# Four pairs of q and k loads, one transposing load and a record load moved in the queues of an attention and mixture-of-experts kernel

## The chip, the cores and the metric

The kernel runs on one core of a Trainium2 chip. The metric is the time of one execution in device microseconds (us). A core has five engines with instruction queues of their own: TensorE (PE in the rows, its weight loads PEld), VectorE (DVE), ScalarE (ACT), GpSimd (POOL) and SyncE (SP). Transfers are started by GpSimd or SyncE and carried out by the 16 DMA engines that the two share.

## The reference

A block-causal attention over 8 batches, 8 heads, 576 rows and head size 64, and on its output a router that sends each of 4608 tokens to two of eight experts:

```python
scores = scale * np.matmul(q, k.transpose(0, 1, 3, 2))      # masked by 64-row blocks
attn = softmax(scores); x = (attn @ v) as [4608, 512]
noisy_logits = x @ w_gate + log1p(exp(x @ w_noise)) * noise
top2, top2_w = two largest of 8, softmax over the two
for e in range(8):
    for k in range(2):
        mask = top2[:, k] == e
        out[mask] += top2_w[mask, k, None] * (relu(x[mask] @ w1[e]) @ w2[e])
```

## The kernel before

**Stages.** The attention goes over four pairs of batches (`g` from 0 to 3). For each pair q and k arrive in five chunks (`load_qk`, chunks 4, 0, 1, 2, 3, each 256 KB but chunk 4), are transposed by TensorE (L439, L444) and copied by VectorE (L460). The scores of a pair are 26 steps (L525, L532, L541), with an exponential on ScalarE after each (L551, L553), then come two sets of nine products with v (L600, L614), which VectorE divides and writes into a row buffer `xr` (L621, L622). The pairs alternate between two such buffers. TensorE then transposes the rows and makes the logits, VectorE ranks the tokens, and `scatter` (L790) sends each row of 512 values and an 8-value record to its expert's region of the DRAM array `xd`, 18 scatters for each pair. Named by the plan, they are `D0.0` to `D0.17` for pair 0, `D1.0` to `D1.17` for pair 1, and so on. Pair 2's division of tile `idx` writes where `D0.2*idx` and `D0.2*idx+1` read, and so waits for these two scatters alone.

Pairs 0 and 1 fill `xd[0]`, pairs 2 and 3 fill `xd[1]`. Each half is then eight buckets, one for each expert with 640 rows, 16 buckets in all (`b` from 0 to 15). For a bucket `load_x` (L934) reads its rows with one transposing DMA into one of three buffers (`xg0`, `xg1`, and `xT`, which lies where the logits' tiles were); buckets 0 and 1 come in tiles instead (L942). TensorE multiplies by w1 (L1017) and w2 (L1033), ScalarE applies the relu (L1023) and copies the result out (L1040, L1042) into one of ten tiles, and SyncE stores each, 128 KB, to `yd` (L1049). GpSimd gathers rows (L1056) and writes the results of the second half (L1075). Weights come by GpSimd's queue (L910, L912).

The records of the second half are read back from `xd[1]` in one transfer of 16-byte pieces (`load_rec`, L974) by SyncE. VectorE works out from them, from L984 on, the weights and addresses that the second half needs.

**Order.** A planner (`Plan`) simulates the engines from written costs and due times and gives one order for everything. Each engine takes its instructions in that order. A transfer may also wait for another that it does not read: each of the two queues marks its transfers on eight semaphores in turn, so one waits until the eighth before it in its queue has landed. `due` of an `LX` step is its place in time for the planner; `LX6.0` is bucket 6, the seventh of the first half.

Of the kernel before, what the change touches and what calls it, by code (L numbers as in the profile page):

```python
# [11 lines left out]
I32 = mybir.dt.int32  # L12
# [200 lines left out]
def kernel(  # L213
# [12 lines left out]
    nc = tc.nc  # L226

    B, H, S, D = q.shape
    N, Dm = out.shape
    E = moe_w_gate.shape[1]  # L230
    F = moe_w1.shape[2]
    assert Dm == H * D and N == B * S
    P = 128
    DB = Dm // P
    FB = F // P
    NG = B // 2
# [4 lines left out]
    CAP = 640  # L241
# [4 lines left out]
    OVB = E * CAP  # L246
    XR = OVB + 2 * TH * P
    DR = Dm + 8
# [12 lines left out]
    xd = [nc.dram_tensor(f"xd{i}", (XR, DR), BF16, kind="Internal").ap() for i in range(NH)]  # L261
# [58 lines left out]
    rc = low.tile([P, E, CT, 4], I32, name="rc")  # L320
# [22 lines left out]
    pl = Plan()  # L343
# [68 lines left out]
    for g in range(NG):  # L412
        for ch in (4, 0, 1, 2, 3):
            for nm in "qk":
                pl.add(f"L{nm}{g}.{ch}", {"POOL": 0.58 if ch == 4 else 0.74}, lambda e, g=g, nm=nm, ch=ch: load_qk(g, nm, ch),
                       due=due_u(g, first_u[ch]) - (18.,18.,18.,22.)[g] + (0.1 if nm == "k" else 0) - (3 if ch == 4 else 0),
                       take=[("r" + nm, ("raw", g, nm, ch))], dma=0.7 if ch == 4 else 1.41, packet=88)
        for i in range(6):
            pl.add(f"V{g}.{i}", {"POOL": 1.18 if i < 4 else 0.7}, lambda e, g=g, i=i: load_v(g, i),
                   due=due_u(g, 6) - (8. if g else 16.) + i * 0.2, rel=0.0 if g < 1 else due_u(g, 0) - 8.,  # L420
                   take=[("vt", ("vt", g))] if i == 0 else [], deps=[f"V{g}.0"] if i else [],
# [55 lines left out]
    for g in range(NG):  # L477
        for nm in "qk":
            for ch in ("4B", 0, 1, 2, 3, "4A"):
# [4 lines left out]
                else:  # L484
                    need, u, lh = [f"L{nm}{g}.{ch}"], first_u[ch], last_h[ch]
                due = due_u(g, u) - 4 + (0.1 if nm == "k" else 0)
# [4 lines left out]
                       take=[("bk", ("tp", g, nm, ch), 1 if g else 0)], free=fr, lat=0.25)  # L491
# [4 lines left out]
                if ch == 0:  # L496
                    pl.add(f"CW{nm}{g}", {"DVE": 0.12}, lambda e, g=g, nm=nm: wrap(g, nm, e),
                           deps=[f"T{nm}{g}.0"] + ([s_name(g - 1, 7)] if g else []), due=due + 0.6, lat=0.15)
                pl.add(f"C{nm}{g}.{ch}", on,
                       lambda e, g=g, nm=nm, ch=ch: turned(g, nm, ch, e), deps=[f"T{nm}{g}.{ch}"] + prev,  # L500
                       due=due + 0.5, free=[("tp", g, nm, ch)], lat=0.15)
# [67 lines left out]
    for g in range(NG):  # L569
        for u in range(UG):  # L570
            st, w = divmod(u, UN)
            hs = [st * SET + w // 3] if w < UN - 1 else range(st * SET, st * SET + SET)
            need = {f"C{nm}{g}.{c}" for h in hs for c in chunks_of(h) for nm in "qk"}
            if 0 in hs:
                need |= {f"CW{nm}{g}" for nm in "qk"}
            small = w == UN - 1
            take = [("sc", ("sc", g, u))]
            pl.add(f"Q{g}.{u}", {"PE": 0.15 if small else (0.26, 0.3, 0.33)[w % 3]},
                   lambda e, g=g, u=u: score(g, u), mode="64*64" if small else "64*128",
                   deps=sorted(need) + ["masks"], due=due_u(g, u), take=take, lat=0.25)  # L580
            pl.add(f"S{g}.{u}", {"ACT": 0.48 if small else 1.0}, lambda e, g=g, u=u: exps(g, u),
                   deps=[f"Q{g}.{u}"], due=due_u(g, u), free=[("sc", g, u)],
                   take=[("esc", ("esc", g, st))] if w == 0 else [], lat=0.2)
# [42 lines left out]
    for g in range(NG):  # L626
        for st in range(2):
            need = [f"S{g}.{st * UN + w}" for w in range(UN)] + [f"V{g}.{i}" for i in range(6)] + ["vones"]
            for idx in range(TG):
                n = 0.75 if idx == 8 else 0.02 + (idx % 4 + 1) * 0.118  # L630
                due = due_u(g, (st + 1) * UN) + 1 + idx * 1.3 - LEAD[g]
                pl.add(f"A{g}.{st}.{idx}", {"PE": n}, lambda e, g=g, st=st, idx=idx: av(g, st, idx),
                       deps=need, due=due, take=[("bk", ("av", g, st, idx))], mode="128*64" if idx == 8 else "128*128",
                       free=[("esc", g, st), ("vt", g)], lat=0.25)
                pl.add(f"N{g}.{st}.{idx}", {"DVE": 0.62}, lambda e, g=g, st=st, idx=idx: av_out(g, st, idx),
                       deps=[f"A{g}.{st}.{idx}"] + ([f"N{g}.0.0"] if (st, idx) != (0, 0) else []), due=due + 0.3,
                       free=[("av", g, st, idx), ("rden", g, st, idx)],
                       take=[("rden", ("rden", g, st, idx))]
# [169 lines left out]
    for half in range(NH):  # L808
        pl.add(f"Z{half}", {"SP": 0.7}, lambda e, half=half: clear_x(half),
               due=due_u(half, 14), rel=due_u(half, 14), deps=["vones"], dma=2.5, packet=165, anchor=True)  # L810

    for g in range(NG):
        half, r0 = g // 2, due_u(g, UG) + 6 - LEAD[g]
        for j in range(5):
# [4 lines left out]
                   take=[("bk", ("xt", g, j))], lat=0.25)  # L819
            pl.add(f"XC{g}.{j}", {"DVE": 0.1 + 0.26 * n, "ACT": 0.12 + 0.44 * n},  # L820
                   lambda e, g=g, j=j: x_turned(g, j, e), deps=[f"X{g}.{j}"], due=d + 0.5,
                   take=[("xT", ("xT", g, j))], free=[("xt", g, j)], lat=0.2)
            pl.add(f"G{g}.{j}", {"PE": 0.11 * n}, lambda e, g=g, j=j: logits(g, j), mode="128*128",
                   deps=[f"XC{g}.{j}", "wgn"] + ([f"G{g}.0"] if j else []) + ([f"R{g - 1}.rows"] if g else []),
                   due=d + 1, take=[("bk", ("lg", g))] if j == 0 else [], free=[("xT", g, j)], lat=0.25)
# [9 lines left out]
               deps=[f"R{g}.cnt", "consts"] + ([f"R{g - 1}.room"] if g else []), due=r1 + 4, free=[("lg", g)])  # L835
        pl.add(f"R{g}.room", {"DVE": 0.4}, lambda e, g=g: room(g), deps=[f"R{g}.rows"], due=r1 + 14)
        pl.add(f"R{g}.keep", {"DVE": 0.6 if g < NG // 2 else 0.2}, lambda e, g=g: keep(g), deps=[f"R{g}.w1", f"R{g}.rows"], due=r1 + 14, free=[("xr", g)])
        for j in range(2 * TG):
            pl.add(f"D{g}.{j}", {"POOL": 1.28}, lambda e, g=g, j=j: scatter(g, j),
                   deps=[f"R{g}.rows", f"R{g}.w1", f"R{g}.tok", f"Z{half}"],  # L840
                   due=(r1 + 7 - 10. if g < NG // 2 else 180. if g == NG - 1 else 150.) + j * 0.9,
# [80 lines left out]
    for e in range(E):  # L922
        b0 = e
        for which in (1, 2):
            for part in range(2):
                deps = freed(e, which)
                pl.add(f"W{which}.{e}.{part}", {"POOL": 0.8}, lambda x, e=e, w=which, p=part: load_w(e, w, p),
                       deps=deps, due=(w_rel[e] if e in w_rel else bucket_due(b0) - 20.) + 4 * which + 2 * part,
# [33 lines left out]
    def rows_of(gs):  # L962
        return [f"D{g}.{j}" for g in gs for j in range(2 * TG)]

    def rows_landed(ins, half, gs):
        own = [i for g in gs for i in scat[g]]
        apart(ins, f"scat{half}", own)
        for i in own:
            tc.add_manual_dep(ins.ins, i.name, SYNC_DEP, reason="rows landed")
        member(ins, f"rows{half}")  # L970
        return ins

    def load_rec():
        ins = nc.sync.dma_start(out=rc.rearrange("p e c w -> p (e c) w"),  # L974
                                in_=xd[1].bitcast(I32)[0:OVB, Dm // 2:DR // 2].rearrange("(c p) w -> p c w", p=P))
        return rows_landed(ins, 1, [2, 3])

    def read_rec():
        f = [rc[:, :, :, i].bitcast(I32 if i == 3 else F32) for i in range(4)]
# [130 lines left out]
    for b, i in ORDER:  # L1110
        half, e = SEQ[b]
        c0, n = PIECES_OF[b][i]
        d0, nb = DUE[(b, i)], step_of(b, i)
        if b < EARLY:
            for c in range(c0 // P, (c0 + n) // P):
                pl.add(f"LX{b}.{c}", {"SP": 0.4}, lambda x, b=b, c=c: load_tile(b, c),
                       deps=rows_of(groups(b, c // 2)), due=d0 - 8 + c * 0.2, take=[("y", ("xl", b, c))], dma=0.4, packet=47)
                pl.add(f"XT{b}.{c}", {"PE": 0.23}, lambda x, b=b, c=c: turn_tile(b, c), mode="128*128", deps=[f"LX{b}.{c}"],
                       due=d0 - 3, take=[("bk", ("xp", b, c), 1)], free=[("xl", b, c)], lat=0.25)
                pl.add(f"XX{b}.{c}", {"DVE": 0.36, "ACT": 0.6}, lambda x, b=b, c=c: tile_turned(b, c, x),  # L1120
                       deps=[f"XT{b}.{c}"], due=d0 - 2, free=[("xp", b, c)], lat=0.2,
                       take=[("xg", ("xg", b))] if c == 0 else [])
                if c:
                    pl.ops[f"XX{b}.{c}"].deps.append(f"XX{b}.0")
        elif i == 0:
            pl.add(f"LX{b}.0", {"SP": 0.3}, lambda x, b=b: load_x(b),
                   deps=rows_of([2 * half, 2 * half + 1]), due=d0 - 12., take=[("xg", ("xg", b))],
                   dma=2.5, packet=22, hold=True, seq="xg")
        for st in range(FB // nb):
            d1 = d0 + st * nb * 0.55 * n / NW  # L1130
            deps = [f"XX{b}.{c}" for c in range(c0 // P, (c0 + n) // P)] if b < EARLY else [f"LX{b}.0"]
            deps = deps + [f"W1.{e}.{p}" for p in range(2)]
            pl.add(f"F1.{b}.{i}.{st}", {"PE": nb * max(0.545 * n / NW, 0.23)},
                   lambda x, b=b, i=i, st=st: layer1(b, i, st), deps=deps, due=d1, mode="128*128",
                   take=[("bk", ("hp", b, i, st), 1)] + ([("h", ("h", b))] if (i, st) == (0, 0) else []),
                   free=[("xg", b)], lat=0.25, seq="layer1")
            pl.add(f"RE.{b}.{i}.{st}", {"ACT": 0.16 + nb * n * 0.001}, lambda x, b=b, i=i, st=st: relu(b, i, st),
                   deps=[f"F1.{b}.{i}.{st}"], due=d1, free=[("hp", b, i, st)], lat=0.2)
        for c in range(CT):
# [6 lines left out]
            for kk in range(2):  # L1146
                deps = []
                for k in need:
# [4 lines left out]
                       due=d2 + kk * 0.87, take=[("bk", ("yp", b, c), 1)] if not kk else [],  # L1153
                       free=[("h", b)], lat=0.25)
            if half == 0 or e < E - 1:
                pl.add(f"Y.{b}.{c}", {"ACT": 0.73}, lambda x, b=b, c=c: keep_row(b, c),
                       deps=[f"F2.{b}.{c}.1"] + (["RR"] if half else []), due=d2 + 1, take=[("y", ("y", b, c))],
                       free=[("yp", b, c)])
                pl.add(f"YS.{b}.{c}", {"SP": 0.6}, lambda x, b=b, c=c: store_row(b, c), deps=[f"Y.{b}.{c}"],
                       due=d2 + 1.5, free=[("y", b, c)], dma=0.4, packet=48)  # L1160
            if half and e:
                deps = ["RR"] + [f"YS.{E + e2}.{c2}" for e2 in range(e) for c2 in range(CT)]
# [160 lines left out]
    pl.eng_free.update({"POOL": 1.5, "DVE": 1.6, "ACT": 2.0, "PE": 1.6, "SP": 1.0})  # L1323
    pl.run()

    reg = {n: nc.gpsimd.to_reg(n - 1) for n in [XR, N] + [e * CAP for e in range(1, E + 1)]}

    sched = tc.manual_schedule(engines={mybir.EngineType.PE, mybir.EngineType.Activation, mybir.EngineType.DVE,
# [122 lines left out]
```

## Time and profile before

| | us |
|---|---|
| median of 3 runs | 459.71 |
| lowest, highest | 459.61, 460.60 |
| the profiled execution, its own time | 462.31 |
| its span, first to last instruction | 460.5 |
| TensorE busy in the span | 400.1 |
| GpSimd busy | 260.1 |
| ScalarE busy | 256.0 |
| VectorE busy | 162.8 |

The profiled execution is one run, 2.60 us above the median; 1.81 us of its time lie outside its span. All times in rows are counted from the span's start. A row's bracket is how long its engine stood idle before it, and what ended that.

### The profile page before, as it was taken

The numbers are of one execution on the slowest core, as the hardware profiler recorded it, in microseconds if no ns is written. First come the engines' busy times: TensorE is split into PE (matmuls) and PEld (weight loads), VectorE is DVE, ScalarE is ACT, GpSimd is POOL, SyncE is SP. The second block draws the span as 40 slices with busy tenths as digits, with TensorE's granted clock in tenths as the row PEclk, the third lists the DMA queues.
The fourth block names the chain that finished last, engine by engine and source line by source line (L and its number), as shares of the span: only waits on it lengthen the run. The fifth ranks groups of instructions, "written<-read, shape, count | busy, mean of one in ns | idle before, by whom it ended". The sixth has DMA issues, their size and how long they took to land. (4 is left out here: it accounts for less than half of the span.)

```text
span 460.5 us, 10885 instructions
## 1 busy us (share of the span) xinstructions
PE 400.1 (87%) x4384; PEld 255.7 (56%) x4384; DVE 162.8 (35%) x451; ACT 256.0 (56%) x447; POOL 260.1 (56%) x293
## 2 busy tenths in 40 slices
PE   3899779869697999999899499999998998999950
PEld 3667666657456776555555165565554554655620
DVE  3768698877617510000000020023322423332320
ACT  2898687957791544745554154555554554655410
POOL 8756447877785775672120002433757777777760
PEclk9999999998999999999999799999999999999995
DMA  8999993999999799999999995758688477555430
GB/s 126 189 218 199 193 187 107 130 204 182 233 163 248 172 217 210 276 236 153 193 220 168 215 154 133 133 128 207 115 172 180 139 182 184 181 176 172 146 129 1
DMA packets 128073, 80.26 MB, mean 174 GB/s; under 512 B 85696, under 2 KB 115981, under 8 KB 128016
## 3 DMA queue, kind: packets, MB, share of 16 engines
q0 software_dynamic: 69856, 52.37, 67.3%
q1 hardware_dynamic: 58160, 27.14, 28.3%
q8 instruction: 36, 0.59, 0.5%
q14 instruction: 21, 0.17, 0.1%
HBM read 72.74 MB, written 35.17 MB: 234 GB/s over the span
## 5 line engine op out<-in xcount | busy, mean ns | idle before, releaser
L551 ACT ACTIVATE esc<-sc 128x1024 bf16<-128x1024 f32 x96 | 92.9, 1028 | 20.5 <-PE sc L532 20.0
L1033 PEld LDWEIGHTS <-h 128*128 128x128 bf16 x640 | 62.2, 98 | 72.7 <-issue 7.6
L790 POOL DMA_INDIRECT xd<-xr,slots x72 | 72.0, 1001 | 37.6 <-issue 17.3
L1023 ACT ACTIVATE h<-sc 128x320 bf16<-128x320 f32 (+1 forms) x120 | 49.6, 444 | 47.2 <-PE sc L1017 30.4
L1056 POOL DMA_INDIRECT xr<-yd,slots x36 | 36.8, 1021 | 66.5 <-DMA yd<-zero 44.8
L1023 ACT ACTIVATE h<-bk 128x320 bf16<-128x320 f32 (+1 forms) x124 | 55.7, 456 | 17.2 <-PE bk L1017 12.6
L1017 PEld LDWEIGHTS <-w 128*128 128x128 bf16 x448 | 40.8, 98 | 15.6 <-issue 1.3
L1017 PEld LDWEIGHTS <-esc 128*128 128x128 bf16 x384 | 37.5, 98 | 20.4 <-issue 3.1
L1056 POOL DMA_INDIRECT xr<-yd,grow x35 | 36.4, 1040 | 17.1 <-issue 9.8
L525 PE MATMUL sc<-qT,kT 64*128 64x512 bf16 (+4 forms) x320 | 37.9, 303 | 4.6 <-ACT esc L551 4.1
L984 DVE TENSOR_TENSOR rtmp<-rc,rowid 128x40 f32<-128x40 f32 x1 | 0.2, 226 | 99.1 <-DMA rc<-xd 99.1
L1033 PE MATMUL sc<-esc,h 128*128 128x512 bf16 x136 | 32.0, 379 | 2.2 <-DVE xr L1069 2.0
L1033 PE MATMUL bk<-w,h 128*128 128x512 bf16 x128 | 31.6, 379 | 0.8 <-DVE xr L1069 0.8
L600 PEld LDWEIGHTS <-esc 128*128 128x128 bf16 x640 | 23.9, 99 | 12.9 <-issue 11.0
L600 PE MATMUL bk<-vt,esc 128*128 128x65 bf16 x540 | 24.4, 197 | 4.3 <-DVE xr L622 1.4
L1033 PE MATMUL sc<-w,h 128*128 128x512 bf16 x112 | 27.6, 379 | 0.2 <-ACT h L1023 0.2
L1075 POOL DMA_INDIRECT out_dram<-xr,trow x21 | 21.4, 1019 | 10.0 <-issue 4.6
L460 DVE COPY kT<-bk 128x1024 bf16<-128x1024 bf16 (+1 forms) x24 | 24.9, 1041 | 5.8 <-PE bk L439 5.1
L1017 PE MATMUL sc<-xg,esc 128*128 128x320 bf16 x168 | 26.6, 299 | 0.4 <-ACT h L1023 0.3
L622 DVE TENSOR_TENSOR xr<-bk,rden 128x256 bf16<-128x256 f32 x61 | 25.9, 424 | 2.1
L1033 PE MATMUL bk<-esc,h 128*128 128x512 bf16 x104 | 24.9, 379 | 1.5 <-DMA esc<-in_moe_w_dram 1.5
L1017 PE MATMUL bk<-xg,esc 128*128 128x320 bf16 x152 | 24.4, 299 | 0.0
(212 smaller groups left out, 640.0 us busy)
## 6 DMA issues: line engine op xcount, KB each, us to landing
w<-in_moe_w_dram POOLq DMA_DIRECT2D x12, 512.0 KB
esc<-in_moe_w_dram POOLq DMA_DIRECT2D x12, 512.0 KB
yd<-xr SPq DMA_DIRECT2D x35, 128.0 KB
rq<-in_q_dram POOLq DMA_DIRECT2D x16, 256.0 KB
rk<-in_k_dram POOLq DMA_DIRECT2D x16, 256.0 KB
vt<-in_v_dram POOLq DMA_DIRECT2D x16, 256.0 KB
yd<-y SPq DMA_DIRECT2D x31, 128.0 KB
out_dram<-o SPq DMA_DIRECT2D x24, 128.0 KB
```

The source lines that it names most:

```text
L460: nc.vector.tensor_copy(o, i)
L525: nc.tensor.matmul(out=sc[:, hf, off:off + z - a], lhsT=kT[sl, c0 + jt * P:c0 + jt * P + P], rhs=qT[sl, c0 + a:c0 + z], start=True, stop=n ...
L551: return nc.scalar.activation(out=esc_t[i][:, hh, :, piece * 512:(piece + 1) * 512], in_=sc, func=AF.Exp, scale=scale)
L600: nc.tensor.matmul(out=a[:, hh, :], lhsT=esc[:, hh, hf, c:c + P], rhs=vb[:, jt, hf, h, 0:D + 1], start=(jt == 0), stop=(jt == ib))
L622: nc.vector.tensor_tensor(out=xr[:, idx, st * SET * D:(st + 1) * SET * D].rearrange("p (h d) -> p h d", h=SET), in0=a[:, :, 0:D], in1=rden ...
L790: ins = nc.gpsimd.indirect_dma_start(out=xd[half].bitcast(I32), out_offset=bass.IndirectOffsetOnAxis(ap=slots[:, g * TG + idx, i:i + 1], a ...
L984: vec.tensor_tensor(out=first, in0=f[0], in1=rowid, op=ALU.is_equal)
L1017: nc.tensor.matmul(out=hp[:, j * n:(j + 1) * n], lhsT=w1sb[:, db, fb * P:(fb + 1) * P], rhs=xg[:, db, c0:c0 + n], start=(db == 0), stop=(d ...
L1023: return nc.scalar.activation(out=h_t[pl.slot(("h", b))][:, s * nb:(s + 1) * nb, c0:c0 + n], in_=bank(("hp", b, i, s))[:, 0:nb * n].rearra ...
L1033: nc.tensor.matmul(out=yp, lhsT=h[:, fb, c * P:(c + 1) * P], rhs=w2sb[:, fb, :], start=(fb == 0), stop=(fb == FB - 1))
L1056: ins = nc.gpsimd.indirect_dma_start(out=g_t[pl.slot(key)], out_offset=None, in_=yd[half][0:len(es) * CAP, :], in_offset=bass.IndirectOffs ...
L1075: ins = nc.gpsimd.indirect_dma_start(out=out, out_offset=bass.IndirectOffsetOnAxis(ap=trow[:, e, c:c + 1], axis=0), in_=out_tile(("o", b, ...
```

## The change

Three edits. After the planner has made its order, the q and k loads of chunks 0, 1, 2 and 3 of the last pair are taken out and put ahead of the scatters `D0.13`, `D0.14`, `D0.16` and `D1.1`. Bucket 6's `LX` step has its due time 44 us ahead of the bucket's instead of 12. The record load becomes two transfers: three experts' records by GpSimd's queue, five by SyncE's.

```diff
     def load_rec():
-        ins = nc.sync.dma_start(out=rc.rearrange("p e c w -> p (e c) w"),
-                                in_=xd[1].bitcast(I32)[0:OVB, Dm // 2:DR // 2].rearrange("(c p) w -> p c w", p=P))
-        return rows_landed(ins, 1, [2, 3])
+
+        q = 3
+        for eng, e0, e1 in ((nc.gpsimd, 0, q), (nc.sync, q, E)):
+            ins = eng.dma_start(out=rc[:, e0:e1].rearrange("p e c w -> p (e c) w"),
+                                in_=xd[1].bitcast(I32)[e0 * CAP:e1 * CAP, Dm // 2:DR // 2].rearrange("(c p) w -> p c w", p=P))
+            rows_landed(ins, 1, [2, 3])
+        return ins
...
-                   deps=rows_of([2 * half, 2 * half + 1]), due=d0 - 12., take=[("xg", ("xg", b))],
+                   deps=rows_of([2 * half, 2 * half + 1]), due=d0 - (44. if b == 6 else 12.), take=[("xg", ("xg", b))],
...
     pl.run()
+
+    for ch, step in ((0, "D0.13"), (1, "D0.14"), (2, "D0.16"), (3, "D1.1")):
+        loads = [pl.ops[f"L{nm}{NG - 1}.{ch}"] for nm in "qk"]
+        pl.order = [o for o in pl.order if o not in loads]
+        i = pl.order.index(pl.ops[step])
+        pl.order[i:i] = loads
```

On GpSimd, around the last scatters of pair 0 (`xd0<-xr0`), before; the v loads of pair 2 are `vt0` and `vt80`, the q and k chunks of pair 3 are `rq` and `rk`:

```order
L397 DMA vt0_144<-in_v_dram 128x16x64 x2
L790 DMA xd0<-xr0_107,slots_101 9728x260
L401 DMA vt80_146<-in_v_dram 64x8x64 x2
L790 DMA xd0<-xr0_107,slots_101 9728x260 x4
L391 DMA rq2_152<-in_q_dram 128x2x512
L391 DMA rk2_157<-in_k_dram 128x2x512
L391 DMA rq3_153<-in_q_dram 128x2x512
L391 DMA rk3_158<-in_k_dram 128x2x512
L391 DMA rq4_154<-in_q_dram 128x2x512
```

and now:

```order
L397 DMA vt0_144<-in_v_dram 128x16x64 x2
L391 DMA rq2_152<-in_q_dram 128x2x512
L391 DMA rk2_157<-in_k_dram 128x2x512
L790 DMA xd0<-xr0_107,slots_101 9728x260
L401 DMA vt80_146<-in_v_dram 64x8x64 x2
L391 DMA rq3_153<-in_q_dram 128x2x512
L391 DMA rk3_158<-in_k_dram 128x2x512
L790 DMA xd0<-xr0_107,slots_101 9728x260 x2
L391 DMA rq4_154<-in_q_dram 128x2x512
L391 DMA rk4_159<-in_k_dram 128x2x512
L790 DMA xd0<-xr0_107,slots_101 9728x260 x2
```

The last five scatters of pair 0 now stand behind two, four or six loads. A little later on GpSimd, among the first scatters of pair 1 (`xd0<-xr1`) and the first weight loads (`w1_0`), before; `rq1` and `rk0` are chunk 3:

```order
L790 DMA xd0<-xr1_108,slots_101 9728x260 x4
L910 DMA w1_0_118<-in_moe_w1_dram 128x2x1024
L790 DMA xd0<-xr1_108,slots_101 9728x260 x3
L910 DMA w1_0_118<-in_moe_w1_dram 128x2x1024
L790 DMA xd0<-xr1_108,slots_101 9728x260
L391 DMA rq1_151<-in_q_dram 128x2x512
L391 DMA rk0_155<-in_k_dram 128x2x512
```

and now:

```order
L790 DMA xd0<-xr1_108,slots_101 9728x260
L391 DMA rq1_151<-in_q_dram 128x2x512
L391 DMA rk0_155<-in_k_dram 128x2x512
L790 DMA xd0<-xr1_108,slots_101 9728x260 x4
L910 DMA w1_0_118<-in_moe_w1_dram 128x2x1024
L790 DMA xd0<-xr1_108,slots_101 9728x260 x3
L910 DMA w1_0_118<-in_moe_w1_dram 128x2x1024
```

Chunk 3 moved ahead of both weight loads and eight scatters, and everything behind `rk0`'s old place keeps its order. On SyncE, after the transposing load of bucket 5 (into `xT`), among the stores of buckets 3 and 4, before:

```order
L1049 DMA yd0<-y3_117 128x512
L1049 DMA yd0<-zero_160 128x512
L1049 DMA yd0<-y0_114 128x512
L1049 DMA yd0<-y1_115 128x512
L1049 DMA yd0<-y2_116 128x512
L1049 DMA yd0<-xr0_107 128x512 x2
L934 DMA_TRANSPOSE xg0_110<-xd0 128x4x640
L1049 DMA yd0<-xr0_107 128x512 x3
```

and now, with the lines of the changed file:

```order
L1053 DMA yd0<-y3_117 128x512
L1053 DMA yd0<-zero_160 128x512
L1053 DMA yd0<-y0_114 128x512
L1053 DMA yd0<-y1_115 128x512
L934 DMA_TRANSPOSE xg0_110<-xd0 128x4x640
L1053 DMA yd0<-y2_116 128x512
L1053 DMA yd0<-xr0_107 128x512 x5
```

Bucket 6's load passed three stores and nothing else. On SyncE the record load stays where it was, with 25 of its 40 pieces for each partition; on GpSimd the other 15 stand behind the last weight load, ahead of the first gather. TensorE, ScalarE and VectorE keep their order.

## Rows read from the trace of the kernel before

**Rows 1.** The page's first part: busy us (share of span), instructions.

```profile
PE 400.1 (87%) x4384; PEld 255.7 (56%) x4384; DVE 162.8 (35%) x451; ACT 256.0 (56%) x447; POOL 260.1 (56%) x293
```

**Rows 2.** TensorE's waits: line, releaser, us in total, times, longest.

```profile
PE sc L1017 <- DMA xg<-xd: 6.8, 1, 6.8
PE bk L439 <- DMA rq<-in_q_dram: 6.0, 4, 2.5
```

**Rows 3.** TensorE's timeline, 85 to 150 us: start, duration, instruction, idle before.

```profile
100.38 0.64 PE L439 MATMUL bk<-ident,rq 128*64 128x128 bf16 x16 [1.20 <-DMA rq<-in_q_dram]
...
102.60 0.64 PE L439 MATMUL bk<-ident,rk 128*64 128x128 bf16 x16 [1.34 <-DMA rk<-in_k_dram]
103.17 2.30 PE L600 MATMUL bk<-vt,esc 128*128 128x65 bf16 x40
...
118.29 0.64 PE L439 MATMUL bk<-ident,rq 128*64 128x128 bf16 x16 [2.48 <-DMA rq<-in_q_dram]
...
140.08 0.92 PE L600 MATMUL sc<-vt,esc 128*128 128x65 bf16 x25 [0.95 <-DMA vt<-in_v_dram]
```

**Rows 4.** Windows: length, busy by engine, granted clock, DMA share, GB/s.

```profile
88.00:92.00 4.00, 2.81 (x61) 2.03 (x61) 3.60 (x15) 3.35 (x6) 3.39 (x5) 1.00 0.38 116
...
100.00:104.00 4.00, 2.28 (x57) 1.99 (x58) 1.99 (x5) 0.38 (x1) 2.10 (x3) 0.91 1.16 288
104.00:112.00 8.00, 7.85 (x165) 6.27 (x164) 6.05 (x18) 5.78 (x7) 6.26 (x7) 0.83 0.91 178
112.00:120.00 8.00, 5.43 (x146) 3.99 (x140) 4.24 (x7) 5.33 (x6) 6.44 (x8) 1.00 1.15 197
```

**Rows 5.** VectorE's timeline, around the turn from pair 2 to pair 3.

```profile
98.16 0.42 DVE L622 TENSOR_TENSOR xr<-bk,rden 128x256 bf16<-128x256 f32 x1
...
103.53 0.18 DVE L621 RECIPROCAL rden<-bk 128x4 f32<-128x4 f32 x1 [1.78 <-PE bk L600]
```

**Rows 6.** GpSimd's timeline, 85 to 150 us.

```profile
89.67 0.98 POOL L790 DMA_INDIRECT xd<-xr,slots  x1 [0.30 <-issue]
90.65 0.78 POOL L391 DMA_DIRECT2D rq<-in_q_dram  x1
...
103.11 0.75 POOL L910 DMA_DIRECT2D w<-in_moe_w_dram  x1 [1.45 <-DMA rk<-in_k_dram]
...
127.78 3.61 POOL L397 DMA_DIRECT2D vt<-in_v_dram  x3
```

**Rows 7.** SyncE's queue, 200 to 300 us: start and duration of the issue.

```profile
215.81 4.13 SPq L1049 DMA_DIRECT2D yd<-y  x3
...
229.32 13.14 SPq L934 DMA_TRANSPOSE xg<-xd  x1
...
260.59 0.40 SPq L974 DMA_DIRECT2D rc<-xd  x1
```

**Rows 8.** TensorE's timeline, 196 to 300 us.

```profile
224.91 1.02 PE L1033 MATMUL bk<-esc,h 128*128 128x512 bf16 x4 [1.47 <-DMA esc<-in_moe_w_dram]
...
252.75 1.03 PE L1033 MATMUL sc<-vt,h 128*128 128x512 bf16 x4
260.54 1.23 PE L1017 MATMUL sc<-xg,qT 128*128 128x320 bf16 x4 [6.77 <-DMA xg<-xd]
...
264.05 0.71 PE L1017 MATMUL bk<-xg,qT 128*128 128x320 bf16 x4
...
280.06 0.71 PE L1017 MATMUL bk<-xg,esc 128*128 128x320 bf16 x4
```

**Rows 9.** SyncE's DMA queue, 226 to 236 us: packets, MB, engine share.

```profile
q1 hardware_dynamic: 1169, 1.02, 39.6%
```

**Rows 10.** ScalarE's timeline, 250 to 264 us.

```profile
252.13 0.60 ACT L1042 ACTIVATE y<-bk 128x512 bf16<-128x512 f32 x1 [2.14 <-PE bk L1033]
```

**Rows 11.** VectorE's first use of the records; GpSimd's first gather.

```profile
269.12 0.23 DVE L984 TENSOR_TENSOR rtmp<-rc,rowid 128x40 f32<-128x40 f32 x1 [99.12 <-DMA rc<-xd]
...
284.86 1.07 POOL L1056 DMA_INDIRECT xr<-yd,slots  x1 [44.77 <-DMA yd<-zero]
```

## The prediction

> **What bounds the kernel now.** I read the share of busy time first: TensorE is busy 400.1 of 460.5 us [rows 1], the other engines little over half, so time is won where TensorE stands idle. The view of its waits comes next, since it says for what. The longest single one is 6.8 us for a transposing load into `xg`, and q loads of chunks 0 to 3 cost 6.0 us in four waits [rows 2]. The timeline then gives the places, and the reader should look at the brackets. The turn from pair 2 to pair 3 has waits of 1.20 and 1.34 us, chunk 3 of the last pair one of 2.48 us, and the last pair's v another of 0.95 us at 140.08 [rows 3]. At 260.54 bucket 6 waits 6.77 us for its rows [rows 8]. From there on TensorE has only waits that its own results lead to, so a shift at 260 us should reach the end.
>
> **First edit, q and k loads.** It adds and removes no transfer. Eight loads pass scatters and some v and weight loads. Upper bound of its gain: the three waits, 1.20 + 1.34 + 2.48 = 5.02 us, and the slow clock behind the first two. The granted clock falls to 0.91 in 100 to 104 us and 0.83 in 104 to 112 us [rows 4], a mixture of the 2.4 and the 1.2 GHz level. By the 0.64 us of the 16 matmuls at 100.38, 40 would take 1.6 us; the 40 at 103.17 took 2.30 [rows 3]. That is 0.7 us there, and with the few behind them I take 0.9. Together 5.9 us.
>
> Not all of it can be had. At the turn VectorE has 1.78 us of idle time only [rows 5], because it must still copy the chunks, so the first two waits give 1.78 + 0.9 = 2.7 us and not 3.4. And there is a new wait. VectorE's last division of the first half, at 98.16 [rows 5], overwrites what `D0.16` and `D0.17` read. `D0.17` was issued at 89.67 [rows 6] and now stands behind six loads at about 0.75 us each of GpSimd's time (0.78 in [rows 6]), so it is issued at about 94.2, four us ahead of the division. Its data queue behind those of the loads. If it lands at once, the wait is nothing. If each load takes 3 us, like the four between the issue at 90.65 [rows 6] and the last chunk's first use at 102.60 [rows 3], six of them, the first issued some 7 us ahead of 89.67, end near 101, and the wait is 3 us. I take 1.2, nearer to the lower end, because the stretch 88 to 92 us has a DMA share of only 0.38 [rows 4]. So the turn gives 1.5 us. Chunk 3's 2.48 us go almost whole, since its loads pass two weight loads and eight scatters, over 10 us of GpSimd's time at 0.98 + 0.30 us a scatter [rows 6]. That is 1.5 + 2.4 = 3.9 us at 120 us.
>
> Then v. TensorE comes to 140.08 that much earlier, and waits there for v already now [rows 3]. So the gain past it is what v gains. Its loads are issued at 127.78, in an order that does not change. GpSimd loses a wait of 1.45 us before the first weight load, which stood for the eighth transfer before it, the k load of chunk 1 [rows 6]; this wait is gone when that load is early. The DMA engines, at shares of 1.16, 0.91 and 1.15 from 100 to 120 us, get (1 - 0.38) x 4 = 2.5 us of work into the hole of 88 to 92 us, and (1 - 0.91) x 8 = 0.7 us into that of 104 to 112 us [rows 4]. I take these 3.2 us as the first edit's gain past 140 us, between 1.5 (GpSimd's wait alone) and 4.9 (the 3.9 and the 0.95 us that stood there). After that scatters, weights and buckets follow TensorE, GpSimd and the queue alike; the one wait on the way, 1.47 us for a weight at 224.91 [rows 8], has no slack, and passes on what the queue has gained.
>
> **Second edit, bucket 6's load.** It is issued at 229.32. Now the third of the three stores that start at 215.81 [rows 7] and the two from `xr` after it stand behind it. SyncE's transfers are served in order, so it starts earlier by the time of three stores. From 226 to 236 us that queue moved 1.02 MB, at a share of 39.6% [rows 9]; three stores of 131 kB take 0.393 / 0.102 = 3.9 us. That is my value. Bounds: nothing, if a transposing load is slower in the new place, and the full 6.77 us. The wait becomes some 2.9 us.
>
> The clock adds to it. From 260.54 to 264.05 three groups of four matmuls took 3.51 us; with the 0.71 us of such a group at 264.05, twice, and the 1.03 of one at 252.75 they would have taken 2.45 at most [rows 8]. So 1.1 us are lost at the 1.2 GHz level after the long wait. After a wait of 2.9 us it may or may not fall: two waits of 2.5 us together brought it down at 103 us, one of 2.48 us at 118 us left the clock at 1.00 [rows 3, 4]. I take half, 0.5, with 0 and 1.1 as bounds.
>
> What is late next: the three stores land only after the load, and their tiles are wanted again by ScalarE. It writes the third tile at 252.13 [rows 10], where the load would still be on its way until about 256. ScalarE would wait there some 5 us. I cost this at nothing because until bucket 6's first product it has nothing else to do, and because the stores are next in the queue, 1.3 us each, so the copies are done before TensorE, which has eight banks, wants theirs back. Without that cover it would be up to 2 us.
>
> **Third edit, records.** One issue of 0.40 us on SyncE [rows 7] stays, and one of about 1.2 us is added on GpSimd (a v load of about as many pieces takes 3.61 / 3 in [rows 6]), where GpSimd then stands idle for 44.77 us [rows 11]. VectorE has the records at 269.12 [rows 11], while they are first needed for the second half's results after 300 us. Bucket 7's rows, behind the records on SyncE, are wanted at 280.06 without a wait [rows 8]. I take 0. If SyncE's part and the ten stores ahead came so late that bucket 7 waited, the edit saves what its 3/8 of the records take of the 8.5 us from issue to use, 3 us; it is the cover for a start 8 us earlier.
>
> **Sum.** 3.2 + 3.9 + 0.5 + 0 = 7.6 us. The profiled execution would fall from 462.31 to 454.7; on the median, which lies 2.60 us lower, it is 459.71 - 7.6 = **452.1 us**.
>
> **Rivals.**
> *The queue eats the first edit.* All of its loads and what they passed use the same DMA engines, with shares of 1.16 and 1.15 at 100 to 104 and 112 to 120 us [rows 4]; v then lands as late as now, TensorE waits longer at 140.08, and only the second edit and the clock are left: 459.71 - 4.4 = 455.3. Against it speaks the 0.38 of 88 to 92 us. The Trainium skill, "DMA: Bandwidth & Descriptors", section "Issuing engines are not separate DMA queues", says that transfers from all issuing engines run on the same 16 DMA engines and interleave there; by that rule an order that leaves no hole smaller gains nothing in the queue, and the time is this rival's. The trace agrees where the share is full and leaves room where it is 0.38.
>
> *Bucket 6's load gains nothing.* It competes with the weights on GpSimd's queue, and a stall of ScalarE on the late stores takes the rest. For it: over 31 us lie between its issue at 229.32 and its use at 260.54 [rows 7, 8], and the weights' queue goes on meanwhile. Against it: three stores less ahead of it are 0.39 MB less in its own queue. Left is the first edit: 459.71 - 3.2 = 456.5.
>
> *Slower: GpSimd falls behind.* Each of the eight moved loads puts a slow landing eight places ahead of some scatter or weight load, and one such wait is 1.45 us in [rows 6]. If all eight cost that, GpSimd and all weights are 11.6 us late; the wait at 224.91 has no slack, nor has bucket 6 then. With 8 us late it is 459.71 + 8 - 3.9 = 463.8. It decides from 3.9 us on. Against it: the loads are older by eight transfers of over 1 us when the wait comes, and one such wait goes away.
>
> *It does nothing that counts.* V and bucket 6 both stay where they are, 459.7.
>
> **Chances and range.** Forecast 0.55 (449.5 to 454.5 by the bounds of its terms, taken not all at once), first edit eaten 0.17, second edit nothing 0.11, nothing at all 0.06, slower 0.08, and 0.03 for more than the forecast. The range is 449.0 to 457.0: it takes in the forecast and the two halves, and leaves out no change and slower, 0.14, and a little at the ends. Faster by over 0.2% (0.9 us, about what three runs that lie within 1 us can tell from no change): 0.55 + 0.17 + 0.11 + 0.03 = 0.86. Same 0.06, slower 0.08.
>
> **What would show it.** On TensorE the waits of 1.34 and 2.48 us are gone, the granted clock is 1.00 in 104 to 108 us, and the product of the last pair with v resumes at about 137. VectorE shows a wait of about 1 us for a scatter at the last division of pair 2's first half; over 3 us there would make the first term wrong. Bucket 6 starts at about 253.5 after a wait of about 3 us, and ScalarE has a wait for a store of `yd` shortly before. Bucket 7 starts without a wait. The last matmul moves by as much as the time. If bucket 6's wait is gone entirely, the second term was too small; if it is still over 5 us, the order of SyncE's queue was not its cause.

## The result and the profile after

Over six runs each the changed kernel takes 449.37 us at the median (447.77 to 450.89), the kernel before 460.51 (459.61 to 462.27). The ratio is 0.9753, with an interval of 0.9722 to 0.9784: some 11.4 us faster, 9.9 to 12.8. The profiled execution took 449.74 us, its span is 448.0 us. The forecast was 452.1 us and 7.6 us faster. Medians here and below are of all executions, while ratios leave out those that the chip ran in a slower state, so the two can differ by up to 1%.

First the page's busy times, and TensorE's waits with their totals, counts and longest, which answer to [rows 1, 2]:

```profile
PE 404.3 (90%) x4384; PEld 258.0 (58%) x4384; DVE 163.2 (36%) x451; ACT 256.6 (57%) x447; POOL 261.4 (58%) x294
```

```profile
PE bk L439 <- DMA rq<-in_q_dram: 2.9, 1, 2.9
PE sc L1021 <- ACT h L1027: 2.2, 4, 1.7
PE sc L1037 <- DVE xr L1073: 2.1, 1, 2.1
PE bk L439 <- issue: 2.1, 2, 1.5
...
PE sc L1021 <- DMA xg<-xd: 1.5, 1, 1.5
```

The wait for `xg` fell from 6.8 to 1.5 us. Of the four q waits one is left, and it lies at the start. (Lines from `load_rec` on are four higher than before.) TensorE's timeline, which answers to [rows 3, 8]:

```profile
9.49 1.06 PE L439 MATMUL bk<-ident,rq 128*64 128x128 bf16 x16 [2.92 <-DMA rq<-in_q_dram]
...
101.68 0.61 PE L439 MATMUL bk<-ident,rq 128*64 128x128 bf16 x16
...
102.61 0.64 PE L439 MATMUL bk<-ident,rk 128*64 128x128 bf16 x16
103.61 0.29 PE L600 MATMUL bk<-vt,esc 128*128 128x65 bf16 x4 [0.36 <-DVE qT L460]
104.73 0.40 PE L600 MATMUL bk<-vt,esc 128*128 128x65 bf16 x8 [0.84 <-DVE kT L460]
105.67 1.36 PE L600 MATMUL bk<-vt,esc 128*128 128x65 bf16 x28 [0.53 <-DVE qT L460]
...
117.76 0.64 PE L439 MATMUL bk<-ident,rq 128*64 128x128 bf16 x16
...
120.94 0.30 PE L439 MATMUL bk<-ident,rk 128*64 128x128 bf16 x4 [1.55 <-issue]
...
140.01 1.42 PE L600 MATMUL sc<-vt,esc 128*128 128x65 bf16 x40
...
251.03 1.03 PE L1037 MATMUL sc<-vt,h 128*128 128x512 bf16 x4
253.59 0.70 PE L1021 MATMUL sc<-xg,qT 128*128 128x320 bf16 x4 [1.54 <-DMA xg<-xd]
...
257.99 0.70 PE L1021 MATMUL sc<-xg,qT 128*128 128x320 bf16 x4 [1.74 <-ACT h L1027]
```

The three waits that the first edit aimed at are gone (101.68, 102.61 and 117.76 have no bracket, nor has v at 140.01, which TensorE reaches no earlier than before). At the turn three waits for VectorE of 1.73 us together stand in their place. Bucket 6 starts after 1.54 us instead of 6.77, then waits 1.74 us for ScalarE. The windows answer to [rows 4]:

```profile
20.00:40.00 20.00, 18.78 (x324) 12.79 (x318) 12.36 (x35) 16.32 (x19) 11.04 (x16) 0.74 1.57 201
100.00:104.00 4.00, 3.46 (x106) 2.97 (x99) 2.61 (x10) 2.04 (x3) 3.09 (x5) 1.00 0.97 145
104.00:112.00 8.00, 6.71 (x119) 5.04 (x119) 7.21 (x20) 3.91 (x5) 6.48 (x8) 0.79 1.00 242
250.00:268.00 18.00, 14.53 (x88) 8.45 (x87) 2.68 (x16) 8.30 (x18) 0.00 (x0) 1.00 1.08 211
```

The granted clock still falls in 104 to 112 us (0.79), and stays at 1.00 at bucket 6. VectorE's last division of the first half [rows 5], ScalarE's third tile [rows 10] and SyncE's queue [rows 7], each in its timeline:

```profile
102.13 0.43 DVE L622 TENSOR_TENSOR xr<-bk,rden 128x256 bf16<-128x256 f32 x1 [1.32 <-DMA xd<-xr,slots]
```

```profile
254.75 0.60 ACT L1046 ACTIVATE y<-bk 128x512 bf16<-128x512 f32 x1 [6.47 <-DMA yd<-y]
```

```profile
215.81 2.69 SPq L1053 DMA_DIRECT2D yd<-y  x2
218.59 20.99 SPq L934 DMA_TRANSPOSE xg<-xd  x1
239.67 0.86 SPq L1053 DMA_DIRECT2D yd<-y  x1
```

All three moved as forecast: VectorE waits 1.32 us for a scatter (forecast 1.2), ScalarE 6.47 us for a store (forecast some 5), and the load is issued 10.7 us earlier. What was not forecast at all lies at the very end. GpSimd's last scatter, before and after:

```profile
445.68 0.98 POOL L1075 DMA_INDIRECT out_dram<-xr,trow  x1 [0.31 <-issue]
```

```profile
440.21 0.98 POOL L1079 DMA_INDIRECT out_dram<-xr,trow  x1 [0.30 <-issue]
```

It ends at 446.66 and at 441.19, 5.5 us earlier. The spans end at 460.5 and 448.0, 12.6 us earlier. So 7.1 us of the gain lie behind the last scatter, 13.9 us of the span before and 6.8 after, where no engine has a row. The trace's records, which hold more than the views show, name two instructions of GpSimd there, a semaphore update of 2.23 us and a drain of 8.40 us before, 0.87 and 2.85 us after.

### The profile page after: what moved, and what is told of

The parts are those of the page before. It is cut to its first block, busy times and chain, and to the rows that moved or that the text cites. A ratio compares the mean times of both kernels' runs of the same rounds, so it can differ in the third digit from the quotient of the medians.

```text
span 448.0 us, 10885 instructions
## 1 busy us (share of the span) xinstructions
PE 404.3 (90%) x4384; PEld 258.0 (58%) x4384; DVE 163.2 (36%) x451; ACT 256.6 (57%) x447; POOL 261.4 (58%) x294
## 4 chain that ended last, share of the span: by engine, by line
PE 44%; POOL 19%; DMA 13%; issue 12%; DVE 9%; ACT 1%; SPq 0%; POOLq 0%; DVEq 0%; ACTq 0%
POOL xr L1060 9%; PE bk L1021 9%; PE sc L1037 8%; PE bk L1037 7%; PE sc L1021 7%; POOL out_dram L1079 6%; PE sc L525 4%; DMA yd<-xr 4%; POOL xd L790 3%; PE bk L439 2%; PE bk L600 2%; DVE kT L460 2%; DMA xr<-yd,grow 2%; DMA xr<-yd,slots 2%; DMA rk<-in_k_dram 2%
## 5 line engine op out<-in xcount | busy, mean ns | idle before, releaser
L525 PE MATMUL sc<-qT,kT 64*128 64x512 bf16 (+4 forms) x320 | 40.1, 318 | 3.8 <-ACT esc L551 3.2
L600 PE MATMUL bk<-vt,esc 128*128 128x65 bf16 x540 | 25.3, 198 | 6.0 <-DVE kT L460 2.1
L1079 POOL DMA_INDIRECT out_dram<-xr,trow x21 | 21.5, 1026 | 11.1 <-DVE xr L1073 4.8
```

The source lines that it names most:

```text
L525: nc.tensor.matmul(out=sc[:, hf, off:off + z - a], lhsT=kT[sl, c0 + jt * P:c0 + jt * P + P], rhs=qT[sl, c0 + a:c0 + z], start=True, stop=n ...
L600: nc.tensor.matmul(out=a[:, hh, :], lhsT=esc[:, hh, hf, c:c + P], rhs=vb[:, jt, hf, h, 0:D + 1], start=(jt == 0), stop=(jt == ib))
L1079: ins = nc.gpsimd.indirect_dma_start(out=out, out_offset=bass.IndirectOffsetOnAxis(ap=trow[:, e, c:c + 1], axis=0), in_=out_tile(("o", b, ...
```

## The experiments

Twelve runs were made, eight of them on another chip, where every kernel, before too, has a median of 528 to 540 us and the same kernel (the third edit alone) gave 1.013 and then 0.987 of before. No time from that chip is used for a size, only its records of the end. TensorE's timeline of the third edit alone shows the difference: groups of a few matmuls with pauses between, in which the engine waits for nothing that the profile shows ("issue").

```profile
68.88 0.30 PE L614 MATMUL bk<-vt,esc 128*64 128x65 bf16 x5 [1.18 <-issue]
70.33 0.34 PE L614 MATMUL bk<-vt,esc 128*64 128x65 bf16 x5 [1.16 <-issue]
```

**Each edit alone, and the change again (the other chip).** `q_only` leaves out the second and third edit, `x_only` the first and third, `r_only` the first and second; `all_again` is the changed kernel. The edit of `x_only` against before:

```diff
-                   deps=rows_of([2 * half, 2 * half + 1]), due=d0 - 12., take=[("xg", ("xg", b))],
+                   deps=rows_of([2 * half, 2 * half + 1]), due=d0 - (44. if b == 6 else 12.), take=[("xg", ("xg", b))],
```

> Only the first edit: the eight q and k loads of the last pair ahead of the scatters. By my sum it is 3.2 us faster than before (range 1.5 to 4.9): no waits for rq and rk at 100 to 103 and 118 us, VectorE waits about 1.2 us at the last division of the first half, and the wait of 6.8 us for xg of bucket 6 stays, which TensorE reaches about 3 us earlier. Rival 1, the queue eats it: 0 us, and TensorE waits 3 to 4 us for v at 137 to 141. Rival 2, it is larger than my term and is most of what the whole change gave beyond 7.6 us: 6 to 7 us, with the weight wait of 1.47 us at 225 us gone as well. Rival 3, the edits work only together: if TensorE only reaches bucket 6 earlier and its load lands where it did, the wait grows to about 10 us and the edit alone gives nothing.

> Only the second edit: bucket 6's load ahead of three stores. By my sum 4.4 us faster (3.9 for three stores and 0.5 for the clock), with a wait of about 3 us left. By the profile of the changed kernel, where the wait was 1.54 us: 6.77 - 1.54 = 5.2, the 1.6 us of the slow clock behind it are had as well, and 1.6 us go to a wait for h while ScalarE catches up on the late stores: 5.2 us. Rival, the load alone gains nothing since the weights hold it up: 0 us, with a wait of over 5 us still.

> Only the third edit: three experts' records in GpSimd's queue. By my sum 0, within 0.2% of before. Rival: the stretch behind the last scatter, 13.8 us in the profile of before and 6.8 in that of the changed kernel, was shortened by this edit: then it is 6 to 7 us faster, and that stretch is about 7 us here and not in the other two single edits.

> The changed kernel once more, for a second profile: 449.4 us, 0.9722 to 0.9784 of before. Two things in its first profile may be accidents of one execution: the wait of 2.92 us for rq at 9.49 us with the slow clock of 0.73 to 0.76 from 20 to 40 us, and only 6.8 us behind the last scatter against 13.8 before. If both are accidents they are gone or different here; if the short end belongs to the change, it is 6 to 7 us again.

Measured: medians of 534.95, 540.02, 539.38 and 536.98 us against 537.58, ratios of 0.992, 1.011, 1.013 and 1.006, which tell nothing, since the third edit alone moved to the other side of 1 when it was repeated there. But the stretch behind the last scatter was 4.35, 13.65, 6.77 and 6.78 us. The short end of the changed kernel is thus no accident of its first profile. The rival of `r_only` holds in its half on the end: the third edit alone brings it to that of the changed kernel. The second leaves it, and the first alone makes it shorter still, which no expectation had.

**The first two edits together, each alone, and a padded kernel (a chip on which before takes 459.44 us).** `q_and_x` is the changed kernel with the old `load_rec`:

```diff
-        q = 3
-        for eng, e0, e1 in ((nc.gpsimd, 0, q), (nc.sync, q, E)):
...
+        ins = nc.sync.dma_start(out=rc.rearrange("p e c w -> p (e c) w"),
```

`before_pad` is the kernel before with one transfer more, into a tile that nothing reads (the line that makes the tile and the two that register the transfer are left out):

```diff
+        pad = nc.gpsimd.dma_start(out=rc2.rearrange("p e c w -> p (e c) w"),
+                                  in_=xd[1].bitcast(I32)[0:3 * CAP, Dm // 2:DR // 2].rearrange("(c p) w -> p c w", p=P))
```

> The first and second edit without the third. What lies behind the last scatter was 13.9 us in before and with the second edit alone, 6.8 in the changed kernel and with the third edit alone, and 4.4 with the first alone. Theory A, the end depends on what GpSimd's queue holds and in which order: this kernel has the queue of the first edit alone, so its end is 4.4 us, and it is 2.4 us faster than the changed kernel, 13.5 us faster than before (0.971). Theory B, the third edit shortens the end and the 4.4 was an accident of one run: the end is 13.9 us, and it is slower than the changed kernel by 7 us, 0.991 of before.

> The first edit alone once more, for a time that can be compared with the change's first one. Theory A: the end of 4.4 us gives 9.5, and what the first edit gives in the body comes on top: 0 (rival: it only lengthens the wait for bucket 6's rows, from 6.8 to about 10 us) to 3.2 us (my term). That is 9.5 to 12.7 us faster, 0.979 to 0.972. If the end is no matter of the program, 0 to 3.2 us faster.

> The second edit alone once more: the end is 13.7 us as in before, and the body gives 4.4 us (my sum) or 5.2 (by the waits in the changed kernel's profile): 0.989 to 0.990. If bucket 6's load gains nothing, 1.000.

> The kernel before, plus one more transfer: GpSimd also loads the records of three experts, into a tile that nothing reads; SyncE still loads all eight. Work is only added. Theory A: what counts is that GpSimd's queue has this transfer of 1920 pieces at this place, so the end shrinks from 13.9 to 6.8 us, and the kernel is 7 us faster than before (0.985). Theory B, the third edit's gain came from SyncE's smaller transfer or from elsewhere: no change, or slower by the 1 us of the added issue.

The stretch behind the last scatter ("end us") is taken off in the last column; the change's own row is from the result, it was not timed beside the others.

| kernel | median us | ratio, interval | end us | us faster | of it in front of the end |
|---|---|---|---|---|---|
| the change | 449.37 | 0.975 (0.972 to 0.978) | 6.78 | 11.4 | 4.3 (2.8 to 5.7) |
| q_and_x | 442.19 | 0.966 (0.961 to 0.971) | 4.54 | 15.7 | 6.4 (4.0 to 8.7) |
| q_only_2 | 448.31 | 0.976 (0.971 to 0.980) | 4.58 | 11.1 | 1.8 (-0.3 to 3.9) |
| x_only_2 | 456.26 | 0.991 (0.987 to 0.995) | 13.60 | 4.1 | 3.8 (2.0 to 5.6) |
| before_pad | 454.76 | 0.992 (0.989 to 0.996) | 6.78 | 3.6 | -3.5 (-5.0 to -2.0) |

("us faster" is one minus the ratio, times before; the last column takes off 13.88 less the end, and so takes the end of the one traced execution for all of its kernel.) Theory A on the end holds in all four: 4.5 us for both kernels with the first edit's queue, 13.6 with the second edit alone, and 6.8 where one transfer was only added. Its time for `before_pad` does not hold: 0.985 was expected, and 0.992 (0.989 to 0.996) came out. The kernel without the third edit is the fastest of all, 442.19 us: the first edit has brought the end to 4.5 us already, and the third, with its 6.8, gives 2.2 us of that back. The last scatter and the span of `q_and_x`:

```profile
435.08 0.97 POOL L1075 DMA_INDIRECT out_dram<-xr,trow  x1 [0.30 <-DVEq L1369]
```

```profile
core 0: 440.6 us, clock 0.981
```

Of `before_pad`, which does more than before and ends earlier behind it (its span of 449.0 less 442.17 is 6.8 us):

```profile
441.19 0.98 POOL L1080 DMA_INDIRECT out_dram<-xr,trow  x1 [0.31 <-issue]
```

Bucket 6 with the first edit alone, the second alone, and both without the third, from TensorE's timelines:

```profile
256.47 1.23 PE L1017 MATMUL sc<-xg,qT 128*128 128x320 bf16 x4 [5.61 <-DMA xg<-xd]
257.49 1.91 PE L1033 MATMUL sc<-vt,h 128*128 128x512 bf16 x4
```

```profile
255.94 0.70 PE L1017 MATMUL sc<-xg,qT 128*128 128x320 bf16 x4 [3.75 <-DMA xg<-xd]
256.48 1.03 PE L1033 MATMUL sc<-vt,h 128*128 128x512 bf16 x4
...
260.33 0.70 PE L1017 MATMUL sc<-xg,qT 128*128 128x320 bf16 x4 [1.73 <-ACT h L1023]
```

```profile
252.84 0.70 PE L1017 MATMUL sc<-xg,qT 128*128 128x320 bf16 x4 [1.83 <-DMA xg<-xd]
...
257.16 0.70 PE L1017 MATMUL sc<-xg,qT 128*128 128x320 bf16 x4 [1.67 <-ACT h L1023]
```

With the first edit alone the wait is 5.61 us and not 10: its load comes earlier with TensorE, so rival 3 of `q_only` is out. Its matmuls behind the wait are still slowed by the 1.2 GHz level (granted clock 0.81 in 250 to 268 us, and 1.23 and 1.91 us, where 0.70 and 1.03 stand with the second edit).

**What moves the end, and the third edit's cost (the other chip).** `all_2` is the change, `q_and_x_2` and `r_only_2` repeat kernels above, and `qx_pad` is `q_and_x` with one small transfer by GpSimd (its tile and two further lines left out):

```diff
+        pad = nc.gpsimd.dma_start(out=rc2,
+                                  in_=xd[1].bitcast(I32)[0:P, Dm // 2:DR // 2].rearrange("(c p) w -> p c w", p=P))
```

> The whole change beside the same without its third edit (next run). Theory A: the third edit costs what it adds to the stretch behind the last scatter, 6.8 against 4.5 us, so the two differ by 2.2 us (0.5%). Theory B: the added transfer of 1920 pieces also costs some us in the body, as the 0.992 of the padded kernel hints, where the shorter end alone would have given 0.985: then they differ by 4 to 6 us (0.9 to 1.3%).

> The first and second edit without the third once more: 0.966 of before again, the end 4.5 us. By theory A 0.5% below the whole change, by theory B about 1%.

> The third edit alone: the end is 6.8 instead of 13.9 us. Theory A, nothing else changes: 7.1 us faster, 0.985. Theory B, the transfer costs 2 to 3 us in the body: 4 to 5 us faster, 0.990. By my prediction's term for it: no change, 1.000.

> The first and second edit, and GpSimd loads besides one small piece of the records (128 pieces of 16 bytes, into a tile that nothing reads) at the place where the third edit loads 1920. If what counts for the end is how many pieces have gone through GpSimd's queue, the end moves a little from 4.5 us, by less than 1 us. If any added transfer there, or the number of transfers, sets it, the end is 6.8 us as with 1920 pieces, and the time 2 us above q_and_x. If the end does not depend on it, 4.5 us and the time of q_and_x.

Measured: 529.55, 533.74, 529.74 and 528.30 us against 533.04, ratios of 0.995, 1.013, 0.987 and 0.982. The change, timed here beside itself without the third edit, was the faster one (0.995, 0.989 to 1.000, against 1.013, 1.006 to 1.021), the opposite of the table above. So what the third edit costs the other two in all is not settled. The two instructions at the end, from the trace's records of all runs:

```
kernel                                    semaphore us  drain us  traces
before, x_only, x_only_2                      2.230      8.398     3
change, all_again, all_2, r_only, r_only_2,
  before_pad                                  0.870      2.845     6
q_only, q_only_2, q_and_x, q_and_x_2          0.420      0.967     4
qx_pad                                        0.440      1.048     1
```

Each pair is the same to the last digit in every trace of its group, on both chips. Without the third edit the order of the loads decides between 0.967 and 8.398 us. With it the order makes no difference: the change and `r_only` both have 2.845. One small transfer more adds 0.020 and 0.081 us, as the first of `qx_pad`'s three expectations has it. In units of that drain step the others stand (2.845 - 0.967) / 0.081 = 23.2 and (8.398 - 2.845) / 0.081 = 68.6 above; with a step known to 0.001 us they may be whole numbers, but this is not shown. They do not follow the number of pieces: 1920 are 15 times 128, and the same 1920 add 23 steps to `q_and_x` and take 68 off before.

## Why the prediction was right, and where not

The direction and the range were right (449.37 us lies just inside its lower bound of 449.0), and so was the mechanism of the second edit. That of the first was right at chunk 3 only. That the sum came near was in part luck: it had 7.6 us in front of the end and nothing behind, and measured were 4.3 and 7.1. The sign "The last matmul moves by as much as the time" failed: it came 6.2 us earlier, the execution was 12.6 us shorter.

**The step that failed: the end of the span has no term, for the third edit ("I take 0") or for the first.** I costed the third edit's issue, its pieces and the wait it covers, all of them in the middle of the run, and never asked what stands between the last scatter and the end of the span, although 13.9 us of it lay there. The end depends on GpSimd's queue: the third edit alone, and a useless transfer at the same place, take 7.1 us off it, the first edit alone 9.3, and the whole change 7.1. Why the queue does so stays open. The "44.77 us" of idle GpSimd as cover was right for the issue (1.22 us at 235.49).

To say where TensorE won and lost in front of the end, here is the start of the same matmul (of 4384, in the same order in all kernels), in us against the profile of before. Each column is one execution and no median: that of `before_pad` took 450.72 us where its median is 454.76, that of before 462.31 where its median is 460.51. So `before_pad` ends 5.23 us ahead here, although its median has lost 3.5 us in front of the end.

| at us in before | change | q_only_2 | x_only_2 | q_and_x | before_pad |
|---|---|---|---|---|---|
| 90.03 | +2.82 | +1.10 | +1.23 | +2.69 | -0.85 |
| 113.06 | +2.02 | +1.16 | -0.65 | +1.88 | -3.09 |
| 119.09 | -0.53 | -1.39 | +1.04 | -0.68 | -3.46 |
| 143.07 | +0.44 | -0.74 | +0.59 | -0.92 | -2.76 |
| 250.16 | -1.72 | -2.91 | -1.58 | -2.76 | +0.80 |
| 270.18 | -6.89 | -3.35 | -4.55 | -7.72 | -1.12 |
| 360.14 | -8.05 | -6.23 | -7.44 | -10.60 | -4.01 |
| 440.11 | -6.23 | -4.16 | -7.33 | -10.20 | -5.23 |

**First edit, 3.2 us.** Mis-sized: from 90 to 143 us the three kernels with it gain 2.38, 1.84 and 3.61 us, mean 2.6, but the two without it gain 0.64 and 1.91, and before is 0, mean 0.85. That leaves 1.8, as the time of `q_only_2` says (1.8, -0.3 to 3.9), inside the 1.5 to 4.9 I gave but not clear of nothing. Chunk 3's 2.4 us were right: from 113 to 119 us all three gain 2.55. At the turn, where 1.5 was forecast, nothing is seen: up to 113 us the three move by -0.80, +0.06 and -0.81, but the two without the edit by -1.88 and -2.24. VectorE's wait was rightly sized (taken 1.2; measured 1.32 in the change, 1.88 and 1.14 in the other two), but TensorE then waits 1.73 us in all for the copies behind it, and the clock, which I had at 1.00 in 104 to 108 us, fell to 0.79 in 104 to 112 us in all three. The waits of 1.20 and 1.34 us in before's profile were also partly that execution's: `x_only_2` has one of 1.11 us there, `before_pad` none over half a us. In the changed kernel a pause of 1.55 us at 120.94 ("issue") gives back part; `q_only_2` has 1.23 there, `q_and_x` 0.23. What causes it is open.

The step to v is the one that was mis-sized. I had its loads come 3.2 us earlier, and TensorE resume at about 137. GpSimd's wait of 1.45 us is gone, but it issues the three loads at 128.19 in the change (127.78 before), at 127.85 in `q_only_2` and 128.09 in `q_and_x`. TensorE comes to the products with v at 138.14 before and 139.64 in the change, so its wait is gone there because it is later. Where TensorE comes as early as before, v still holds it up, in `q_only_2` and `q_and_x`:

```profile
128.19 3.60 POOL L397 DMA_DIRECT2D vt<-in_v_dram  x3
```

```profile
139.34 0.92 PE L600 MATMUL sc<-vt,esc 128*128 128x65 bf16 x25 [0.20 <-DMA vt<-in_v_dram]
```

```profile
139.15 0.92 PE L600 MATMUL sc<-vt,esc 128*128 128x65 bf16 x25 [0.25 <-DMA vt<-in_v_dram]
```

Against 140.08 that is 0.7 to 0.9 us for v, not 3.2. The holes that I counted as the queue's room, up to a share of 1, were no measure of it: the share goes to 1.57 in 20 to 40 us, and in 88 to 92 us it rose from 0.38 to 1.44. The weight's wait of 1.47 us at 225 us, which I had passing on the queue's gain, is gone too; but it is gone in `x_only_2` as well. (Counted from 90 to 250 us instead of 143, the same difference of means is therefore 4.3 us, and 1.9 against `x_only_2` alone.)

**Rival "the queue eats the first edit".** It does not hold as a whole: v gained 0.7 to 0.9 us, and the edit 1.8 in front of the end, between the rival's 0 and my 3.2. The Trainium skill, "DMA: Bandwidth & Descriptors", section "Issuing engines are not separate DMA queues", has transfers run on the same 16 DMA engines whichever engine started them. No run here tests that rule on the first edit, since the loads that it moves and the scatters that they pass are all started by GpSimd.

**Second edit, 3.9 + 0.5 us.** Right. From 250 to 270 us the three kernels with it gain 5.17, 4.96 and 2.97, the two without 0.44 and 1.92, before 0; the means differ by 3.6, and `x_only_2` is 3.8 us faster in front of the end. The wait left is 1.54 us in the change and 3.75 with the second edit alone, where 2.9 was forecast; the clock's loss goes entirely, and in return "I cost this at nothing" was wrong for ScalarE's stall: TensorE then waits 1.74, 1.73 and 1.67 us for it (the change, the second edit alone, `q_and_x`). That is the 2 us I named for the case without cover: the copies of ScalarE's backlog stand ahead of the relu that TensorE needs.

**The sum.** Without the third edit the body gains 6.4 us (4.0 to 8.7), by the single edits 1.8 + 3.8 = 5.6; the 7.6 lie inside. With it the body gains 4.3 (2.8 to 5.7). `before_pad` loses 3.5 us of body (2.0 to 5.0) to its added transfer, so the third edit may cost the body some 2 us; the intervals overlap, and it is not shown. The profiles show the changed kernel behind `q_and_x` in 270 to 440 us: it gains 1.72 less up to 360, and loses 1.82 against 0.40 behind that. The second loss is the clock's. After a wait for VectorE the matmuls are slow in the change (granted clock 0.72 in 382 to 388 us) and not in `q_and_x`:

```profile
382.79 1.70 PE L1037 MATMUL sc<-esc,h 128*128 128x512 bf16 x4 [2.14 <-DVE xr L1073]
```

```profile
380.51 1.02 PE L1033 MATMUL sc<-esc,h 128*128 128x512 bf16 x4 [2.41 <-DVE xr L1069]
```

But `q_only_2`, which loses 2.07 us there, has the same slow matmuls (1.87 us after a wait of 2.67) without the third edit. The forecast "Bucket 7 starts without a wait" held.

## What to carry to other kernels

Read the span from its end as well: compare the last row of any engine with the span, and ask of every edit to GpSimd's queue what it does to that stretch, since here the largest single effect lay there. Before a wait is priced, see whether a second execution has it; two of the three waits that the first edit was to win were partly one execution's. That a wait is gone is no gain by itself: look whether the engine comes to that place earlier or later. A load moved ahead of stores in SyncE's queue gains the time of the stores, and hands a wait to the engine whose tiles the stores were to free: check what that engine does first when it resumes.

## What the hardware showed that was not expected

GpSimd's last drain and the semaphore update ahead of it took 1.4 to 10.6 us by what had stood in its queue of transfers and, without the third edit, in which order, exactly repeatable, with 0.1 us for one small transfer more. That the same 1920 pieces add 23 steps in one kernel and take off 68 in another could come from a count that starts over at some point; that is argued from the numbers, and no experiment here shows what is counted or that point.

By 80 us, up to where all kernels have the same order, the profiles differed by 3.7 us (+2.82 to -0.84, nearly as in the table's first row): the first q loads land at different times, and in two of the profiles the granted clock is 0.74 in 20 to 40 us, in the others 1.00.

The other chip needs 528 to 540 us for the same kernels. The idle of TensorE put down to "issue" is 34 to 46 us in its eight profiles and 1.5 to 4.8 us in the other six; the same kernel has 42.5 us there as `q_and_x_2` and 1.5 as `q_and_x`.
